# Banded attention with a hand-fixed TensorE order: work moved between ScalarE, VectorE and GpSimd, one PSUM bank used twice, and the theta product started five steps later

## The chip, the cores and the metric

The kernel runs on one core of one Trainium2 chip. The metric is the device time of one execution in microseconds (us). Three runs of the kernel before took 623.08, 624.20 and 625.01 us, so the median is 624.2 us.

Engines are named as the profile names them: PE is TensorE (PEld its weight loads), DVE is VectorE, ACT is ScalarE, POOL is GpSimd, SP is SyncE, which here only issues DMAs.

## The reference

Three blocks run one after the other on batch 2, sequence 768, width 512 (8 heads of 64).

1. Attention: scores = q·kT / 8, kept where the key is one of the first `n_sink` keys (4 here) or lies in the window of the last 128 positions, then softmax, then the product with v. Its output, heads side by side, is x, twelve tiles of 128 rows by 512.
2. Token mixing: theta = x·w_theta; zr = x·cos(theta), zi = x·sin(theta); y = w_tok_r·zr + w_tok_i·zi; u = x + y; u + relu(u·w_ch).
3. The real part of a 2-D Fourier transform of that, added to it, a layer norm, and an MLP of width 2048.

Weights come as 64-bit floats, and the kernel turns their words into 32-bit floats itself. Products that need more than one rounded factor are done as three products of a high and a low part (hi·hi, hi·lo, lo·hi).

## The kernel before

The attention stage (`attn_banded`, L610) is one loop over steps `s`, four per tile of 128 queries (`n, hp = divmod(s, 4)`; twelve tiles, so 48 steps, and a few more for what trails). The loop writes down the order of all work on PE by hand: `strict` (L228) makes every PE instruction follow the one before it in the program. The other engines' queues are ordered by a planner that puts an instruction in its queue when the planner's own clock finds it ready. In one step stand, in this order on PE:

- on even `s` the scores of four heads (`score_mms`, L483), into four PSUM banks; DVE adds the mask and finds the row bound (L515), ACT takes the exponential (L519), and the bank is free again when the exponential has read it;
- on `s % 4 == 2` the product with v of the tile of six steps ago (`av`, L561) into the single bank of the ring `ps_acc` (profile name `oa`), copied to `oT` by ACT (L586);
- for `0 < s < first(0)` two products of a tile of zeros (L641), which nothing reads;
- the transposes of two heads' probabilities (`turn`, L531) into one of the two banks of the ring `ps_tp` (profile name `tp`), copied out in turn by ACT and DVE (L552);
- on `s % 4 == 1`, for tiles that have earlier sink keys, one more transpose: the 16 sink columns of all heads, gathered by a copy `psk` (L524, ACT), also go to a `tp` bank (L555) and are copied to `pst`;
- on `s % 4 == 3` the transpose back of the finished product (`av_turn`, L588), also into a `tp` bank, which DVE reads to normalise (L601);
- parts of `theta_gen` (L776): first four transposes of a finished x tile into a `tp` bank, then twelve products over the following steps into the bank `th`.

`theta_gen` copies its `tp` bank twice on ACT: once rounded to the PE's reduced type (`hi`, L784) and once in full (`xT`, L786). POOL, or DVE for the last tiles, subtracts the two (`lo`, L787). After the products ACT scales the result to turns (`ph`, L798), DVE adds and subtracts a large constant to round to whole turns (`km`, L799 and L800), and POOL subtracts (L801).

Tile u's theta begins at step `first(u) = 4u + 5 + max(4, T0 - u)`. With `T0 = 7` this is 12, 15, 18, 21 and then every fourth step from 25.

The stage also converts weights: at steps 5, 7, 9, 11 (`THS`) the four quarters of w_theta, each split into high and low a step later, and then every third step from 15 to 39 a piece of the token weights (`P0B`, `P0E`, L687). A conversion (`conv`, L269) is one ACT instruction (L281) and three DVE instructions (L289, L290, L293), or, where `low_act` is set, two on ACT (L281, L284) and two on DVE (L285, L293); `low_act` is not set in this stage. Converting a piece also asks SP for the next one. The DMAs of k, q and v are asked for a tile ahead.

After the attention `rest` (L1199) runs the token mixing of the first batch (`y_gen`, from about 168 us in the profile), and then everything else, which the change does not touch.

Of the kernel before, what the change touches and what calls it, by code (L numbers as in the profile page):

```python
# [15 lines left out]
ALU = mybir.AluOpType  # L16
# [5 lines left out]
BLK = 128 + SINK  # L22
PW = 256 + SINK
BIG = 8.0e9
MAGIC = 12582912.0
# [4 lines left out]
GROUPS = [0, 3, 1, 2]  # L30
NSLOT = 67
NSLOT2 = 8
T0 = 7
DEPTH = 3
NRAW = 3
NJIT = 12
# [3 lines left out]
C1E = 12  # L40
TLC = 1
WN = 7
P0B = 15
P0N = 3
P0E = 40
F0 = 0
F1 = 2
ETH = 9
# [3 lines left out]
T1 = 4  # L52
TD = 1
AH = 5
THS = (5, 7, 9, 11)
P1E = 11
P2F = 1
TL = 2
# [132 lines left out]
class _Body:  # L191
# [315 lines left out]
    def scores(self, n, hp):  # L507
        nc = self.nc
        i, c = self.seq[n][1], n % 3
        nb, sm, p = self.tn[n]  # L510
        wd = PW if i else 128
        mask = self.masks[min(i, 2) if c else (0, 1, 3)[min(i, 2)]]
        for u, sc in enumerate(self.scs.pop((n, hp))):
            h = 2 * hp + u
            nc.vector.tensor_tensor_reduce(  # L515
                out=sc[:, 0:wd], in0=sc[:, 0:wd], in1=mask, op0=ALU.add, op1=ALU.min,
                scale=-0.125, scalar=3.0e38, accum_out=nb[:, h:h + 1],
            )
            self.last_exp = nc.scalar.activation(  # L519
                p[:, h, 0:wd], sc[:, 0:wd], AF.Exp, bias=nb[:, h:h + 1], scale=-1.0, accum_out=sm[:, h:h + 1]  # L520
            ).ins
        if hp == 3 and i >= 2:
            psk = self.psk.next()
            self.rnd("a", psk, p[:, :, 128:BLK])  # L524
            self.pt[n, 5] = psk
        if hp == 3:
            q = self.q.pop(n)
            if n:
                self.give(q)

    def turn(self, n, hp):  # L531
        nc = self.nc
        b, i = self.seq[n]
        c = n % 3
        p = self.tn[n][2]
        tp = self.ps_tp.next().rearrange("p (a m) -> p a m", a=4)
        pt = self.take(4, 128)
        parts = []
        for u in range(2):
            x, y = p[:, 2 * hp + u, 0:128], p[:, 2 * hp + u, BLK:PW]  # L540
            if i:
                prev, cur = (x, y) if c else (y, x)
                parts.append((u, prev, n - 1))
                parts.append((u, cur, n))
            else:
                parts.append((u, x, n))
        k = len(parts)
        for a, (u, pp, _) in enumerate(parts):
            self.tr(tp[:, a, :], pp, self.ident)
            yield  # L550
        tail = 4 * n + hp >= 4 * len(self.seq) - 5
        self.ev[n, hp] = self.rnd("v" if tail else EPT[hp], pt[:, 0:k], tp[:, 0:k])  # L552
        self.pt[n, hp] = pt, [(u, m) for u, _, m in parts]
        if hp == 3 and i >= 2:
            tp = self.ps_tp.next()  # L555
            self.tr(tp[:, 0:128], self.pt.pop((n, 5)).rearrange("p h c -> p (h c)"), self.ident)
            pst = self.pst.next()
            self.ev[n, 4] = self.rnd("v" if tail else "a", pst, tp[:, 0:128])
            self.pt[n, 4] = pst
# [26 lines left out]
        self.rnd("a", self.oT, acc)  # L586

    def av_turn(self, n):  # L588
        tp = self.ps_tp.next().rearrange("p (a m) -> p a m", a=4)
        for a in range(4):  # L590
            self.tr(tp[:, a], self.oT[:, a], self.ident)
        self.give(self.oT)
        self.normalize(*self.seq[n], tp.rearrange("p a m -> p (a m)"), self.tn.pop(n)[1])
# [16 lines left out]
    def attn_banded(self):  # L610
        last = len(self.seq) - 1
        nc = self.nc
        self.tn, self.pt, self.scs, self.ev = {}, {}, {}, {}
        th = {}
        self.zth = self.ps_th.tiles[0]
        first = lambda u: 4 * u + AL + 2 + max(T1, T0 - u // TD)
        nstep = 4 * (last + 1)
        for s in range(nstep + T0 + AL + 4):
            n, hp = divmod(s, 4)
            if n < last and hp == 0:  # L620
                b, i = self.seq[n]
                if n:
                    self.load_k(n + 1)
                    self.load_q(n + 1)
                    self.load_v(n + 1)
                if i == NS - 2 and b + 1 < B:
                    self.load_sink(b + 1)
            if s == nstep - 4:
                self.sz = self.s.carve(6)
            if s == AH:  # L630
                self.ahead(2)
            if n <= last and not s % 2:
                self.score_mms(n, hp)
            g, k = divmod(s - AVS, 4)
            if 0 <= g <= last and k == 0:
                self.av(g)
            turn = self.turn(*divmod(s - TL, 4)) if TL <= s < nstep + TL else iter(())
            if 0 < s < first(0):

                for _ in range(2):  # L640
                    i = nc.tensor.matmul(  # L641
                        self.zth[:, 0:256], lhsT=self.zz[:, 0:128], rhs=self.zz, start=s == 1, stop=False,
                        skip_group_check=True,
                    ).ins
                    self.chained(i)
            for _ in turn:
                pass
            g, k = divmod(s - AVS, 4)
            if 0 <= g <= last and k == 1:
                self.av_turn(g)  # L650
            if n <= last and not s % 2:
                self.scores(n, hp)
                self.scores(n, hp + 1)
            if s in (nstep + 1, nstep + 3):
                u = (s - nstep) // 2
                with self.paced(ref=self.ev[last, 0]) if u else self.tc.issue_after(self.last_exp):
                    self.trig_act(0, u)
                with self.paced(ref=self.tl if u else self.ev[last, 1]):
                    self.trig_mul(0, u, "v")
            for u in range(last):  # L660
                k = s - first(u)
                if k == 0:
                    for _ in th.pop(u - 1, ()):
                        pass
                    th[u] = self.theta_gen(*self.seq[u])
                if 0 <= k < 4:
                    next(th[u], None)
            if n < last:
                if s in MST:
                    with self.paced(ref=self.last_exp):  # L670
                        self.build_mask(1 + MST.index(s))
                if s == SKS:
                    with self.paced(ref=self.last_exp):
                        self.sink_cols(0, 0, 1, 2)
                if hp == 0:
                    if n == 1:
                        with self.paced():
                            self.sink_v(0)
                    elif n and self.seq[n][1] == 0:
                        self.sink_cols(b, 0, 1)  # L680
                        self.sink_v(b)
            if s in THS:
                self.pump(0, lag=0, ref=self.last_exp)
            elif s - 1 in THS:
                with self.paced(ref=self.last_exp):
                    self.weight_split("th", THS.index(s - 1))
            elif P0B <= s < P0E and s % P0N == 0:  # L687
                self.pump(12, lag=0, ref=self.last_exp)
            if s - nstep in TAIL:
                u = TAIL.index(s - nstep)  # L690
                with self.paced(ref=self.ev[last, u]):
                    self.weight_split("tok", 1, (0, 2, 1)[u])
                if u < 2:
                    self.pump(8, ref=self.tl)
            if nstep - 4 <= s < nstep - 1:
                with self.paced(ref=self.last_exp):
                    self.weight_split("tok", 0, s - nstep + 4)
        for l in th.values():
            for _ in l:
                pass  # L700
        self.pump(8, ref=self.nrm)
        self.marks, self.strict = [], False
# [73 lines left out]
    def theta_gen(self, b, i):  # L776
        nc = self.nc
# [3 lines left out]
            self.tr(tp[:, a, :], x[:, a * 128:(a + 1) * 128], self.ident)  # L781
        hi = self.take(4, 128, dt=F32R)
        lo = self.take(4, 128, dt=F32R)
        self.rnd("a", hi, tp)  # L784
        xt = self.xT[b][:, :, i * 128:(i + 1) * 128]
        nc.scalar.activation(xt, tp, AF.Copy)  # L786
        self.low("v" if 6 * b + i >= ETH else "p", lo, xt, hi)  # L787
        self.tl = nc.cur_bb.bb.instructions[-1]
        yield
        th = self.ps_th.next()  # L790
# [5 lines left out]
        self.give(hi, lo)  # L796
        ph, km = self.take(512), self.take(512)
        nc.scalar.activation(ph, th, AF.Copy, scale=INV2PI)  # L798
        nc.vector.tensor_scalar(km, ph, MAGIC, None, op0=ALU.add)  # L799
        nc.vector.tensor_scalar(km, km, MAGIC, None, op0=ALU.subtract)  # L800
        nc.gpsimd.tensor_tensor(ph, km, ph, op=ALU.subtract)  # L801
        self.give(km)
        self.ph[b, i] = ph
# [569 lines left out]
```

## Time and profile before

| | value |
|---|---|
| median of three runs | 624.2 us |
| the profiled execution | 624.34 us |
| its span, first to last instruction | 622.6 us |
| PE busy | 587.7 us (94%) |
| DVE busy | 351.0 us (56%) |
| ACT busy | 349.0 us (56%) |
| POOL busy | 299.0 us (48%) |
| mean granted TensorE clock | 0.985 of full |

A row of a window says how long the stretch is, how long each engine was busy in it (with the count of instructions), and the granted clock as a share of full speed (0.50 is 1.2 GHz, 1.00 is 2.4 GHz). A row of the timeline gives start, duration, engine, line, operation and tiles; what stands in square brackets is how long the engine sat idle before it and whose instruction ended that. L206, L207, L211, L221 and L226 are helpers (a copy on ACT, a copy on DVE, a subtraction, a product, a transpose), so there the tile names tell which is which.

### The profile page before, as it was taken

The page shows a single profiled execution, that of the slowest core. Times are in us where ns is not written, and L with a number is a line of the kernel's source. Part 1 is how long each engine was busy: PE and PEld are TensorE (multiplying, and loading weights), DVE is VectorE, ACT ScalarE, POOL GpSimd, SP SyncE. Part 2 cuts the span into 40 slices and gives each one's busy share as a digit, 9 for nine tenths or more (in the row PEclk, how much of TensorE's full clock was granted, in tenths as well). Part 3 has the DMA queues.
Part 4 walks back from the last instruction along what each step waited for, and adds up shares of the span by engine and source line. Part 5 has one row for each costly group of instructions (what it writes and reads, how often), then busy time and mean ns, then how long its engine had stood idle before and what let it go on. Part 6 is the DMA issues. An engine that isn't in the chain of part 4 may idle for free.

```text
span 622.6 us, 9732 instructions
## 1 busy us (share of the span) xinstructions
PE 587.7 (94%) x3586; PEld 511.5 (82%) x3586; DVE 351.0 (56%) x713; ACT 349.0 (56%) x787; POOL 299.0 (48%) x252
## 2 busy tenths in 40 slices
PE   8879999797999999998999999999999999999996
PEld 6647776575787899987899999999898999989995
DVE  5766777667899859896366765548333411121112
ACT  4656657577676554647577775436548534333340
POOL 1121312123367652524665755666856566556551
PEclk9989999799899999999999999999999999999999
DMA  7733433120042722550026652100000100010001
GB/s 245 273 119 99 122 113 109 39 83 1 1 136 69 215 65 68 157 149 1 1 68 204 193 160 88 51 1 1 0 1 4 49 1 1 1 52 1 1 1 57
DMA packets 23338, 46.63 MB, mean 75 GB/s; under 512 B 2512, under 2 KB 9552, under 8 KB 23280
## 3 DMA queue, kind: packets, MB, share of 16 engines
q1 hardware_dynamic: 22032, 43.74, 22.3%
q0 software_dynamic: 1248, 2.17, 1.2%
q8 instruction: 30, 0.49, 0.3%
q14 instruction: 28, 0.23, 0.1%
HBM read 42.75 MB, written 3.15 MB: 74 GB/s over the span
## 4 chain that ended last, share of the span: by engine, by line
PE 61%; DVE 5%; ACT 1%; POOL 1%; issue 0%; POOLq 0%; ACTq 0%
PE pc L221 24%; PE acc L221 20%; PE s L221 8%; PE bank L221 7%; PE s L226 2%; ACT t L206 1%; POOL t L211 1%; DVE t L211 1%; DVE t L1146 0%; DVE t L819 0%; DVE t L987 0%; DVE t L999 0%; ACT t L1068 0%; DVE t L995 0%; DVE t L1053 0%
## 5 line engine op out<-in xcount | busy, mean ns | idle before, releaser
L211 POOL TENSOR_TENSOR t<-t 128x512 fp32r<-128x512 f32 x151 | 203.5, 1367 | 177.6 <-ACT t L206 153.4
L221 PE MATMUL acc<-t 128*128 128x512 f32 x648 | 178.5, 394 | 0.0
L206 ACT ACTIVATE t<-t 128x512 fp32r<-128x512 f32 x172 | 102.4, 626 | 71.5 <-PE acc L221 26.5
L221 PEld LDWEIGHTS acc<-t 128*128 128x128 f32 x648 | 116.5, 188 | 17.8
L221 PE MATMUL pc<-t 128*128 128x384 f32 (+1 forms) x672 | 124.9, 314 | 1.0 <-POOL t L211 0.6
L221 PEld LDWEIGHTS pc<-t 128*128 128x128 f32 x672 | 113.8, 188 | 11.1 <-POOL t L211 0.8
L1133 DVE SCALAR_TENSOR_TENSOR t<-pc,t 128x384 fp32r<-128x384 f32 x64 | 35.6, 557 | 123.9 <-ACT t L1132 123.7
L211 POOL TENSOR_TENSOR t<-xT,t 128x512 fp32r<-128x512 f32 x39 | 52.3, 1359 | 99.6 <-ACT xT L786 61.6
L221 PE MATMUL s<-t 128*128 128x256 f32 (+3 forms) x492 | 70.3, 286 | 1.6 <-DVE st L1053 0.8
L221 PE MATMUL pc<-uh,t 128*128 128x384 f32 x256 | 70.6, 337 | 0.0
L221 PEld LDWEIGHTS s<-t 128*128 128x128 f32 x492 | 65.8, 190 | 4.9 <-DVE st L1053 1.0
L221 PE MATMUL bank<-t 128*128 128x512 f32 x216 | 65.2, 398 | 1.4 <-DVE t L211 1.4
L1132 ACT ACTIVATE t<-pc 128x384 fp32r<-128x384 f32 x64 | 31.3, 489 | 60.8 <-PE pc L221 56.8
L281 ACT ACTIVATE raw<-raw 128x512 f32<-128x512 f32 x58 | 38.8, 674 | 15.1 <-DMA raw<-in_w_ch_dram 9.4
L221 PEld LDWEIGHTS pc<-uh,t 128*128 128x128 f32 x256 | 46.2, 188 | 0.8
L221 PEld LDWEIGHTS bank<-t 128*128 128x128 f32 x216 | 38.7, 188 | 8.0 <-DVE t L211 2.3
L221 PE MATMUL pc<-ul,t 128*128 128x384 f32 x128 | 43.0, 336 | 0.6 <-DVE ul L211 0.6
L519 ACT ACTIVATE p<-sc,nb 128x272 f32<-128x272 f32 (+1 forms) x72 | 33.2, 467 | 16.7 <-DVE nb L515 16.1
L221 PE MATMUL th<-t 128*128 128x512 f32 x132 | 42.5, 438 | 0.0
L515 DVE CUSTOM_DVE_ANT_0 sc<-sc,m 128x272 f32<-128x272 f32 (+1 forms) x72 | 28.9, 442 | 7.4 <-PE sc L221 7.3
L206 ACT ACTIVATE t<-xT 128x512 fp32r<-128x512 f32 x36 | 21.0, 625 | 19.1 <-PE acc L221 7.4
L226 PE MATMUL tp<-ident,p 128*128 128x128 f32 x176 | 29.5, 289 | 2.2 <-ACT t L206 1.8
(142 smaller groups left out, 826.0 us busy)
## 6 DMA issues: line engine op xcount, KB each, us to landing
raw<-in_w_ch_dram SPq DMA_DIRECT2D x36, 512.0 KB, 3.9
kst<-in_k_dram SPq DMA_DIRECT2D x12, 256.0 KB, 3.8
t<-in_v_dram SPq DMA_DIRECT2D x12, 256.0 KB, 4.2
raw<-in_w_tok_rT_dram SPq DMA_DIRECT2D x6, 512.0 KB, 3.6
raw<-in_w_tok_iT_dram SPq DMA_DIRECT2D x6, 512.0 KB, 3.6
out_dram<-t SPq DMA_DIRECT2D x12, 256.0 KB, 2.7
t<-in_q_dram SPq DMA_DIRECT2D x11, 256.0 KB, 3.7
raw<-in_w_theta_dram SPq DMA_DIRECT2D x4, 512.0 KB, 6.0
```

What stands on the lines that cost most here:

```text
L206: return nc.scalar.activation(o, i, AF.Copy).ins
L211: e.tensor_tensor(o, x, hi.bitcast(F32), op=ALU.subtract)
L221: i = self.nc.tensor.matmul(o, lhsT=lhsT, rhs=rhs, start=start, stop=stop, skip_group_check=True).ins
L226: self.chained(self.nc.tensor.transpose(o, x, ident).ins)
L281: nc.scalar.activation(hf, hf, AF.Copy, scale=2.0 ** -112)
L515: nc.vector.tensor_tensor_reduce(out=sc[:, 0:wd], in0=sc[:, 0:wd], in1=mask, op0=ALU.add, op1=ALU.min, scale=-0.125, scalar=3.0e38, accum_ ...
L519: self.last_exp = nc.scalar.activation(p[:, h, 0:wd], sc[:, 0:wd], AF.Exp, bias=nb[:, h:h + 1], scale=-1.0, accum_out=sm[:, h:h + 1]).ins
L1132: nc.scalar.activation(hh, hp, AF.Relu)
L1133: self.hl = nc.vector.scalar_tensor_tensor(hl, in0=hp, scalar=0.0, in1=hh.bitcast(F32), op0=ALU.max, op1=ALU.subtract).ins
```

## The change

- `T0` from 7 to 12: theta of tile u begins at 17, 20, 23, 26, 29, 32, 35, 38, 41, and every fourth step from 45. Tile 0 begins five steps later, tile 7 one step later, tile 8 and those after it as before. The products of zeros run while `s < first(0)`, so through step 16 where it was step 11.
- `THS` to 6, 9, 12, 15; `P0B`, `P0E` to 18 and 43: the nine token pieces are converted at 18 to 42 where it was 15 to 39.
- `low_act` is set for steps below 18, so that the four quarters of w_theta take the form with two ACT and two DVE instructions.
- The sink columns are gathered by POOL where it was ACT.
- The sink transpose and the transpose back take the bank of `ps_acc` where they took one of `ps_tp`.
- For the first nine tiles theta's `hi` is a POOL copy of `xT` where it was an ACT copy of the `tp` bank.
- The rounding to whole turns is one POOL instruction where it was two on DVE.

```diff
-T0 = 7
+T0 = 12
-P0B = 15
+P0B = 18
-P0E = 40
+P0E = 43
-THS = (5, 7, 9, 11)
+THS = (6, 9, 12, 15)
...
-            self.rnd("a", psk, p[:, :, 128:BLK])
+            nc.gpsimd.tensor_copy(psk, p[:, :, 128:BLK])
...
         if hp == 3 and i >= 2:
-            tp = self.ps_tp.next()
+            tp = self.ps_acc.next()
...
     def av_turn(self, n):
-        tp = self.ps_tp.next().rearrange("p (a m) -> p a m", a=4)
+        tp = self.ps_acc.next().rearrange("p (a m) -> p a m", a=4)
...
+            self.low_act = s < P0B
             if s in THS:
...
-        self.rnd("a", hi, tp)
         xt = self.xT[b][:, :, i * 128:(i + 1) * 128]
+        late = 6 * b + i >= ETH
+        if late:
+            self.rnd("a", hi, tp)
         nc.scalar.activation(xt, tp, AF.Copy)
-        self.low("v" if 6 * b + i >= ETH else "p", lo, xt, hi)
+        if not late:
+            nc.gpsimd.tensor_copy(hi, xt)
+        self.low("v" if late else "p", lo, xt, hi)
...
         nc.scalar.activation(ph, th, AF.Copy, scale=INV2PI)
-        nc.vector.tensor_scalar(km, ph, MAGIC, None, op0=ALU.add)
-        nc.vector.tensor_scalar(km, km, MAGIC, None, op0=ALU.subtract)
+        nc.gpsimd.tensor_scalar(km, ph, MAGIC, MAGIC, op0=ALU.add, op1=ALU.subtract)
         nc.gpsimd.tensor_tensor(ph, km, ph, op=ALU.subtract)
```

## Rows read from the trace of the kernel before

**Rows 1.** Windows: attention, two stretches of it at a low clock, and what follows
```profile
7.10:168.20 161.10, 138.63 (x1059) 106.16 (x1058) 114.17 (x334) 104.06 (x313) 37.89 (x31) 0.95 0.34 110
41.00:49.00 8.00, 7.15 (x48) 4.84 (x48) 2.80 (x11) 4.52 (x15) 2.51 (x2) 0.59 0.06 16
113.00:120.00 7.00, 6.73 (x26) 4.72 (x27) 2.55 (x10) 2.72 (x11) 0.00 (x0) 0.55 0.08 30
168.20:200.00 31.80, 30.38 (x169) 25.69 (x168) 31.49 (x38) 22.58 (x42) 21.23 (x13) 1.00 0.32 100
```
**Rows 2.** Waits of PE in attention, the largest: total us, times, longest
```profile
PE tp L226 <- ACT t L206: 18.3, 15, 4.0
```
**Rows 3.** Groups by line and shape, attention: transposes into `tp`; idle before them last
```profile
L226 PE MATMUL tp<-ident,psk 128*128 128x128 f32 x8 | 2.8, 352 | 3.4 <-ACT t L206 2.6 <-ACT xT L786 0.8
L226 PE MATMUL tp<-ident,t 128*128 128x128 f32 x92 | 15.0, 287 | 14.7 <-ACT t L206 13.9 <-ACT xT L786 0.8
```
**Rows 4.** Timeline of PE, five waits in attention
```profile
22.83 0.65 PE L226 MATMUL tp<-ident,t 128*128 128x128 f32 x4 [1.69 <-ACT t L206]
...
28.77 0.95 PE L221 MATMUL sc<-kst,t 64*128 64x272 f32 x5 [1.36 <-ACT p L519]
...
40.93 1.11 PE L226 MATMUL tp<-ident,p 128*128 128x128 f32 x4 [1.80 <-ACT t L206]
...
66.16 0.65 PE L226 MATMUL tp<-ident,t 128*128 128x128 f32 x4 [0.79 <-ACT xT L786]
...
113.27 1.11 PE L226 MATMUL tp<-ident,t 128*128 128x128 f32 x4 [3.40 <-ACT t L206]
```
**Rows 5.** Timeline of ACT: copies of `oT` and of a `tp` bank
```profile
20.17 0.59 ACT L206 ACTIVATE t<-oa 128x512 f32<-128x512 f32 x1
...
22.18 0.60 ACT L206 ACTIVATE t<-tp 128x512 f32<-128x512 f32 x1
...
111.94 0.59 ACT L206 ACTIVATE t<-oa 128x512 f32<-128x512 f32 x1
```
**Rows 6.** Timeline of DVE and POOL ahead of the wait at 113
```profile
107.27 1.30 DVE L800 TENSOR_SCALAR t<-t 128x512 f32<-128x512 f32 x1
...
106.99 1.30 POOL L211 TENSOR_TENSOR t<-xT,t 128x512 fp32r<-128x512 f32 x1 [8.36 <-ACT xT L786]
```
**Rows 7.** Timeline of PE, steps 8 and 9: zeros and transposes
```profile
24.53 1.13 PE L641 MATMUL th<-z 128*128 128x256 f32 x4
25.50 0.60 PE L226 MATMUL tp<-ident,p 128*128 128x128 f32 x4
25.94 1.03 PE L641 MATMUL th<-z 128*128 128x256 f32 x4
26.80 0.60 PE L226 MATMUL tp<-ident,p 128*128 128x128 f32 x4
```
**Rows 8.** Timeline of PE, ACT and POOL: theta of tile 1, three steps behind tile 0
```profile
53.42 0.60 PE L226 MATMUL tp<-ident,t 128*128 128x128 f32 x4
...
55.48 0.94 PE L221 MATMUL th<-t 128*128 128x512 f32 x3
...
54.60 0.60 ACT L786 ACTIVATE xT<-tp 128x512 f32<-128x512 f32 x1
...
55.28 1.39 POOL L211 TENSOR_TENSOR t<-xT,t 128x512 fp32r<-128x512 f32 x1 [10.82 <-ACT xT L786]
```
**Rows 9.** Groups by line and shape: what is moved, and the nearest prices on POOL
```profile
L800 DVE TENSOR_SCALAR t<-t 128x512 f32<-128x512 f32 x10 | 7.9, 792 | 0.0
L799 DVE TENSOR_SCALAR t<-t 128x512 f32<-128x512 f32 x10 | 4.4, 442 | 6.1 <-ACT t L798 6.0
L801 POOL TENSOR_TENSOR t<-t 128x512 f32<-128x512 f32 x10 | 12.7, 1273 | 5.6 <-DVE t L800 4.4 <-PE oa L221 0.8 <-PE tp L226 0.4
L1072 POOL TENSOR_SCALAR rstd<-mv 128x1 f32<-128x1 f32 x12 | 2.3, 190 | 10.2 <-ACT t L1070 7.2 <-ACT mv L1066 1.6 <-ACT xT L1070 0.9
L284 ACT ACTIVATE raw<-raw,below 128x512 int32<-128x512 uint32 x33 | 24.9, 756 | 0.0
```

## The prediction

> **What bounds the kernel now.** I read the windows first, then PE's waits, then the groups by shape, then the timeline around each wait. The reader is to see in the windows that attention runs from 7.1 to 168.2 us, that PE is busy for 138.63 of its 161.10 us, and so idle for 22.5, at a mean granted clock of 0.95 [rows 1]. Behind it PE hardly stops: 30.38 of the next 31.8 us. All that the change touches lies in attention or trails into that stretch, so the question is how much of the 22.5 us, and of what the low clock costs, goes away. The low clock stands in two places above all: 41 to 49 us at 0.59, a loss of 8 × 0.41 = 3.3 us, and 113 to 120 us at 0.55, 7 × 0.45 = 3.2 us [rows 1]; PE had paused 1.80 us just before the first and 3.40 us before the second [rows 4].
>
> The waits say who is late: 18.3 us in 15 pieces, PE's transposes waiting for an ACT copy [rows 2]. By shape it is two kinds: the eight sink transposes 3.4 us, and the transposes of `t` (the transpose back and theta's) 14.7 us [rows 3]. The order on PE is fixed, so one transpose without a bank holds everything behind it. At 22.83 the transpose back starts 1.69 us late; its operand `oT` was copied at 20.17 + 0.59 = 20.76, and what it got at last was the copy of a `tp` bank, at 22.18 + 0.60 = 22.78 [rows 4, 5]. So that wait is for a bank and not for data.
>
> **The change part by part.** The sum is made against the profiled execution, 624.34 us (span 622.6, 1.74 outside it); the median of the runs, 624.2, is the same within 0.14.
>
> *The transposes in the `oa` bank.* The ring `tp` keeps only the probabilities and theta. The sink transpose no longer needs a `tp` bank: 3.4 us gone [rows 3]. The transpose back waits only for `oT`, which it needs anyway. Of the 14.7 us I count whole the waits that were for a bank: 1.69, 0.79 [rows 4] and three more of the latter's pattern, 1.3 together; 3.8 in all. In three others `oT` itself was late, as at 113.27: it was there at 111.94 + 0.59 = 112.53, 0.74 before PE began [rows 4, 5]. About 0.55 each, 1.7. Together 5.5; the longest wait, 4.0 [rows 2], I leave. What does the shared bank cost? `av` writes it again three steps after the transpose back was put there and one step after the sink transpose; scores and a probability transpose stand between them on PE. I take 0; if ACT is late with that copy, `av` stalls, at most as the sink transposes do now (0.4 us each).
>
> *Theta later, its weights spread out, the low word on ACT.* Steps 5 to 11 now hold a conversion every other step, and step 12 theta's first transposes. The wait of 1.36 us for an exponential at 28.77 and the one of 1.80 at 40.93 [rows 4] are of that stretch: 3.2 us. With no theta before step 17 the two `tp` banks serve the probabilities alone, and with them should go the low clock of 41 to 49, 3.3 us. The four quarters cost ACT 4 × 0.756 = 3.0 us more [rows 9], hidden by ACT's idle time (57 of 161 us [rows 1]); uncovered it would be those 3.0. DVE loses one instruction of each. SP's refills move with the conversions; the DMAs are busy for 0.34 of the time [rows 1], so I count nothing.
>
> *Zeros.* Steps 12 to 16 get two products each. In steps 8 and 9 they took 25.50 − 24.53 = 0.97 and 26.80 − 25.94 = 0.86 us of PE [rows 7]. Five steps × 0.92 = 4.6 us **added**; theta's own PE work is only moved, into a phase with a theta every three steps.
>
> *Rounding and `hi` on POOL.* No row has POOL with one input of 128x512. From below 0.19 (128x1), from above 1.27 (two inputs of 128x512) [rows 9]. The nearest in size is the upper one; with one operand less I take the middle, 0.7. DVE gets back 7.9 + 4.4 = 12.3 us in attention [rows 9], ACT nine copies of 0.6 [rows 8] and eight short ones. DVE matters where it delays an exponential and thereby ACT's queue: at 107.27 the second rounding instruction stood 1.30 us, until POOL's at 106.99 ended (its own work is 0.4) [rows 6], then a weight conversion in the same way, and the 3.40 us wait and the low clock followed. What is left of these two is 2.7 + 3.2 = 5.9. A conversion still falls there and POOL is fuller, so I take half: 2.9.
>
> The price is theta's chain. Now the products follow ACT's `hi`; after, ACT's `xT` and then POOL's copy: from the end of the transposes at 54.02 to the end of `xT` at 55.20 it is 1.18, less some 0.5 for the copy of `hi` that stood ahead of it, 0.7; then 0.08 to POOL [rows 8], 0.7 for the copy, 0.08 back: 1.56 us. What PE has to do in that time depends on the step. Transposes at `s % 4 == 1` are followed by scores and `av`: enough. At 3 scores and one transpose, 55.48 − 54.02 = 1.46 [rows 8]: wait 0.1. At 2 two transposes of 0.44 [rows 7]: 0.7. At 0 one and the sink transpose: 1.05. Beginning at 20, 23, 26, 32, 35, 38, theta meets each of these twice: 2 × (0.1 + 0.7 + 1.05) = 3.7 us **added**, with 1.0 (POOL at its lower bound, 0.5 quicker) and 7.1 (at its upper, 0.57 slower) as ends. Thetas 9 to 11 keep ACT's `hi`.
>
> *Density.* Steps 17 to 41 hold more per step. From below 0: a theta three steps behind the one before ran without a wait of PE [rows 8]. From above 4.9, the three early waits again [rows 4]. Nearer to the former, with fuller queues: 2.0 added.
>
> **Sum.** Gone 3.4 + 5.5 + 3.2 + 3.3 + 2.9 = 18.3; added 4.6 + 3.7 + 2.0 = 10.3. Net −8.0: 624.3 − 8.0 = **616 us**. Behind attention I count nothing: DVE is busy 31.49 of 31.80 us there [rows 1], but its work is set off by PE's progress and shifts with it.
>
> **A rule weighed.** At 107.27 a DVE instruction with its operands in SBUF stood until POOL's ended [rows 6], so POOL time is not free for DVE. The Trainium skill, "SBUF — State Buffer", section "Who interferes with whom", calls this an exclusive lock on one pair of ports, which speaks against moving work from DVE to POOL. By that rule the new POOL work shuts DVE out for about as long as DVE is relieved: this is rival 3. On POOL's price the same skill, "GPSIMD Engine Reference", section "4.1 Engine selection", calls one-input work roughly line-rate; by its 1.03 cycles an element (section 3.1) I estimate 0.44 us and a little, which would take some 1 us from the sum; no row here shows it.
>
> **The rivals.**
> 1. *Theta's `hi` late on POOL* (slower). Where a theta begins, POOL gets the rounding and the subtraction of the tile before at the same moment. If the planner puts both ahead of `hi`, it comes 0.7 + 1.27 later, of which 0.5 had passed: about +1.5 at each of six thetas, +8.9. PE then pauses over 2.5 us at steps 20 and 32, and pauses of that kind went ahead of the low clock [rows 1, 4]: +3.2 twice. 616 + 8.9 + 6.4 = 631. It decides from about 1.3 us more per theta (8.0 / 6) on. For: the queue is strictly in order, and `hi` is now on PE's path. Against: at 55.28 POOL, idle for 10.82 us, took the new tile's `lo` first, so ahead of the old tile's subtraction [rows 8].
> 2. *DVE freed for good* (faster). The whole 5.9 us around 113 go, `hi` is hidden behind other waits, and half of the longest wait (4.0 [rows 2]) goes too: 616 − 3.0 − 3.7 − 2.0 = 607. For: DVE's chain led to the wait at 113 [rows 6]. Against: the longest one lies where ACT starts on the sines, and DVE has no part in it.
> 3. *DVE not freed*. New POOL time in attention is 10 × 0.7 + 9 × 0.7 + 8 × 0.35 (half a copy) = 16 us against 12.3 that DVE gets back. Then the 2.9 us stay and about 2 us of new exponential waits come: 621. For: a POOL instruction held DVE for its whole length [rows 6]. Against: it held one whose operands lie in SBUF; DVE's score and copy instructions read PSUM.
> 4. *Given back behind attention*. If DVE's 31.49 of 31.80 us there is a bound of its own, whose start doesn't move, the time stays near 624. Against: PE was idle for only 31.80 − 30.38 = 1.4 us of it.
>
> **How the numbers follow.** About 0.3% (1.9 us) is what a measurement of this kernel can tell from no change. Forecast 0.42 (its own range 611 to 621), rival 1 0.17, rival 2 0.18, rival 3 0.11, rival 4 0.12. Rival 4 is no change; rival 1 and a little of 3 slower; so faster 0.70, same 0.12, slower 0.18. For 8 in 10 I leave out the outer parts of rivals 1 and 2: 605 to 627.
>
> **What would show it.** After: no wait of PE before the sink transposes; the transpose back starting right behind the copy of `oT`; no low clock around 41 us; 64 records of zeros where there were 44; the first theta product at steps 21, 24, 27, 33, 36, 39 waiting for a POOL copy, by 0.1 to 1.05 us each; attention ending near 160. Wrong if POOL's one-input instructions take over 1 us, if PE's waits for POOL sum to more than 8 us, or if the next stage gets longer by what attention loses.

## The result, and the profile after

The changed kernel takes 630.6 us (629.0 to 632.5, four runs) where the kernel before takes 624.5 (623.1 to 625.0). The ratio is 1.0103, with a 95% interval of 1.0070 to 1.0136: slower by 1%, outside the range that was forecast (605 to 627). The profiled execution took 629.0 us, its span is 627.2.

The loss lies in attention and nowhere else. At the end of the first token mixing DVE adds a product to `xT`, four times in a run. The row of these instructions gives shortest, median and longest duration, then the first and the last start. Before:

```profile
L865 DVE TENSOR_TENSOR xT<-pc,xT x4: 679/680/682, 222.8 to 313.7; 128x512 f32<-128x512 f32 x4
```

After, where the line is L869:

```profile
L869 DVE TENSOR_TENSOR xT<-pc,xT x4: 679/680/681, 227.4 to 318.3; 128x512 f32<-128x512 f32 x4
```

The first comes 4.6 us later, and from it to the end of the span it is 399.8 us in both (622.6 − 222.8, 627.2 − 227.4). What follows attention only shifts.

The windows of after, against [rows 1] (duration, busy time of PE, PEld, DVE, ACT and POOL, granted clock, DMA):

```profile
7.10:172.60 165.50, 142.27 (x1071) 109.91 (x1068) 101.13 (x307) 99.16 (x300) 63.52 (x56) 0.95 0.33 108
64.00:71.00 7.00, 6.56 (x42) 4.89 (x43) 2.19 (x10) 2.13 (x9) 3.15 (x4) 0.53 0.41 127
90.00:94.00 4.00, 3.75 (x14) 2.40 (x15) 1.53 (x7) 0.93 (x4) 2.69 (x3) 0.63 0.18 70
111.00:115.00 4.00, 3.17 (x11) 2.02 (x11) 0.45 (x2) 0.00 (x0) 3.26 (x4) 0.57 0.38 131
```

Attention is 4.4 us longer although DVE has 13 us less to do in it and ACT 5 us less; POOL has 26 us more. PE is idle for 23.2 us, where it was 22.5. The low clock hasn't gone but moved: 41 to 49 us runs at full speed now, and 64 to 71, 90 to 94 and 111 to 115 don't.

PE's waits in attention, against [rows 2], say what took the place of ACT:

```profile
PE th L221 <- POOL t L791: 13.8, 6, 3.4
PE tp L226 <- ACT t L206: 4.2, 3, 1.8
PE oa L226 <- ACT t L206: 2.4, 1, 2.4
PE sc L221 <- ACT p L519: 2.2, 2, 1.4
PE oa L221 <- DVE t L207: 0.3, 1, 0.3
```

The 18.3 us for ACT's copies fell to 6.6 (4.2 + 2.4). In their stead stand six waits of theta's products (`th`) for POOL's L791, which is the copy that makes `hi`. The groups of transposes, against [rows 3], show that the part with the banks did what it says: no wait is left before the sink transposes, and the transposes of `t`, now half in `oa` and half in `tp`, wait for 5.3 us where it was 14.7 (the busy time comes first, the idle time before the group behind the second bar).

```profile
L226 PE MATMUL oa<-ident,t 128*128 128x128 f32 x44 | 6.8, 278 | 2.6 <-ACT t L206 2.4
L226 PE MATMUL tp<-ident,t 128*128 128x128 f32 x44 | 6.7, 275 | 2.7 <-ACT t L206 2.7
L226 PE MATMUL oa<-ident,psk 128*128 128x128 f32 x8 | 2.2, 272 | 0.0
```

Now one theta, that of tile 1, in the timeline of after: PE, ACT and POOL.

```profile
59.92 0.60 PE L226 MATMUL tp<-ident,t 128*128 128x128 f32 x4
...
64.44 1.65 PE L221 MATMUL th<-t 128*128 128x512 f32 x3 [3.34 <-POOL t L791]
...
61.17 0.61 ACT L803 ACTIVATE t<-th 128x512 f32<-128x512 f32 x1
61.65 0.62 ACT L789 ACTIVATE xT<-tp 128x512 f32<-128x512 f32 x1
...
61.88 1.94 POOL L804 TENSOR_SCALAR t<-t 128x512 f32<-128x512 f32 x1 [7.92 <-ACT t L803]
63.78 0.60 POOL L791 CAST t<-xT 128x512 fp32r<-128x512 f32 x1
64.36 1.26 POOL L805 TENSOR_TENSOR t<-t 128x512 f32<-128x512 f32 x1
65.58 1.28 POOL L211 TENSOR_TENSOR t<-xT,t 128x512 fp32r<-128x512 f32 x1
```

`xT` is there at 61.65 + 0.62 = 62.27 and POOL's copy needs 0.60, so `hi` could be there before 63. But ACT gave POOL tile 0's `ph` 0.5 us earlier, and POOL began its rounding (L804), which lasts 1.94 us. `hi` starts at 63.78, right behind it, and PE at 64.44. The same four instructions in the same order stand at each of the eight thetas of tiles 1 to 8 (at tile 8 a `psk` copy stands between them); PE waits at six of them, and at tiles 4 and 8 it doesn't. The rounding is not the whole wait: behind a free POOL `hi` would have started 0.07 us after `xT` (run 3 below has 62.88 and 62.95), at 62.34, so 1.4 of the 3.34 us are the queue's. Over the six waits this makes 8.4 of the 13.8 us (an estimate from the starts of the copies). The rest is the longer path over `xT`, which was late itself: its transposes ended at 59.92 + 0.60 = 60.52, and ACT had an exponential, an instruction of a weight conversion and `ph` ahead of it. The prices on POOL, over the whole run:

```profile
L804 POOL TENSOR_SCALAR t<-t 128x512 f32<-128x512 f32 x12 | 24.6, 2047 | 44.9 <-ACT t L803 44.9
L805 POOL TENSOR_TENSOR t<-t 128x512 f32<-128x512 f32 x12 | 16.8, 1404 | 0.2
L791 POOL CAST t<-xT 128x512 fp32r<-128x512 f32 x9 | 5.5, 607 | 0.6 <-ACT xT L789 0.6
L524 POOL COPY psk<-p 128x128 f32<-128x128 f32 x8 | 2.3, 291 | 20.6 <-ACT p L519 20.5
```

The copies cost a little less than was taken (0.61 for 0.7, 0.29 for 0.35). The rounding costs 2.05 us where 0.7 was taken, and lies outside the bounds that [rows 9] gave, 0.19 to 1.27.

### The profile page after: what moved, and what is told of

Read it like the earlier page. It is cut to its first block, busy times and chain, and to the rows that moved or that the text cites. A ratio compares the mean times of both kernels' runs of the same rounds, so it can differ in the third digit from the quotient of the medians.

```text
span 627.2 us, 9817 instructions
## 1 busy us (share of the span) xinstructions
PE 591.7 (94%) x3606; PEld 516.1 (82%) x3606; DVE 339.7 (54%) x685; ACT 344.0 (55%) x774; POOL 331.1 (53%) x281
## 4 chain that ended last, share of the span: by engine, by line
PE 73%; DVE 10%; ACT 8%; issue 3%; DMA 2%; POOL 2%; SPq 0%; ACTq 0%; DVEq 0%; POOLq 0%
PE pc L221 24%; PE acc L221 21%; PE s L221 8%; PE bank L221 8%; PE th L221 3%; ACT p L519 3%; PE oa L221 2%; ACT t L206 2%; PE s L226 2%; PE tp L226 2%; PE sc L221 2%; DMA raw<-in_w_theta_dram 1%; DVE t L211 1%; DVE t L823 1%; POOL t L804 1%
## 5 line engine op out<-in xcount | busy, mean ns | idle before, releaser
L211 POOL TENSOR_TENSOR t<-t 128x512 fp32r<-128x512 f32 x151 | 202.7, 1363 | 172.1 <-ACT t L206 145.5
L211 POOL TENSOR_TENSOR t<-xT,t 128x512 fp32r<-128x512 f32 x39 | 52.6, 1367 | 27.8 <-ACT t L206 27.7
L221 PE MATMUL th<-t 128*128 128x512 f32 x132 | 41.9, 440 | 13.9 <-POOL t L791 13.8
L804 POOL TENSOR_SCALAR t<-t 128x512 f32<-128x512 f32 x12 | 24.6, 2047 | 44.9 <-ACT t L803 44.9
L221 PEld LDWEIGHTS th<-t 128*128 128x128 f32 x132 | 23.8, 202 | 18.6 <-POOL t L791 15.6
```

The lines of the kernel that those rows point to most:

```text
L211: e.tensor_tensor(o, x, hi.bitcast(F32), op=ALU.subtract)
L221: i = self.nc.tensor.matmul(o, lhsT=lhsT, rhs=rhs, start=start, stop=stop, skip_group_check=True).ins
L804: nc.gpsimd.tensor_scalar(km, ph, MAGIC, MAGIC, op0=ALU.add, op1=ALU.subtract)
```

## The experiments

The theory from here on is *the queue*: `hi` stands behind a 2 us rounding in POOL's queue, PE's fixed order waits for it, and behind the pause the clock is low. Its rivals are *POOL's load* (its new instructions shut DVE out, wherever they stand) and *the schedule* (theta every three steps, more products of zeros). Each run is compared with the kernel before on the same chip (624.1 to 625.2 us); the changed kernel is the 630.6 us above.

**1. `hi` on ACT again, all else as changed.**

```diff
-        if late:
-            self.rnd("a", hi, tp)
+        self.rnd("a", hi, tp)
         nc.scalar.activation(xt, tp, AF.Copy)
-        if not late:
-            nc.gpsimd.tensor_copy(hi, xt)
```

> The changed kernel with one part undone: theta's high part is again an ACT copy of the transposes' bank. Queue theory (the 2 us rounding stands ahead of the high part in POOL's queue, and PE waits for it): the 13.8 us of PE's waits for POOL go, and most of the 6 us of low clock behind them; some of it comes back as other waits, so 614 to 619 us. Rival 'POOL's load' (its 25 us of rounding shut DVE out): the rounding stays, so at least 627. Rival 'schedule' (theta every three steps and ten more products of zeros cost it): at least 627.

608.4 us, ratio 0.9742 (0.9714 to 0.9770). One copy per theta on the other engine is worth 22 us, and without it the change is a gain of 16; that is more than the queue expected (614 to 619). The waits of PE:

```profile
PE oa L226 <- ACT t L206: 3.0, 2, 2.4
PE tp L226 <- ACT t L206: 2.6, 2, 1.8
PE th L221 <- ACT t L206: 2.5, 2, 1.3
PE sc L221 <- ACT p L519: 1.9, 3, 1.0
PE s L226 <- DVE t L601: 0.5, 1, 0.5
```

The windows from 62 to 122 us and from 122 to 150 here, and then the first of them in the changed kernel:

```profile
62.00:122.00 60.00, 57.12 (x455) 44.61 (x456) 39.21 (x124) 39.80 (x125) 30.89 (x24) 1.00 0.32 102
122.00:150.00 28.00, 25.55 (x218) 20.67 (x217) 19.85 (x48) 22.78 (x55) 17.23 (x14) 0.94 0.06 20
```

```profile
62.00:122.00 60.00, 48.32 (x337) 36.49 (x337) 30.39 (x91) 26.53 (x85) 26.14 (x23) 0.89 0.25 82
```

POOL is busier here than in the changed kernel (30.89 against 26.14 us), with PE at 57.12 of 60 us and the full clock. POOL's load and the schedule are both refuted as the main cause: both are in this kernel, but for the 5.5 us of POOL's copies themselves. The first `xT<-pc` comes at 206.3 us of a span of 606.3, so 400.0 us before the end: the gain too is attention's alone. Of all the kernels run here this one (with run 7, which is the same within the measurement) is the fastest, and the version to keep.

**2. The rounding back on DVE, `hi` on POOL.**

```diff
-        nc.gpsimd.tensor_scalar(km, ph, MAGIC, MAGIC, op0=ALU.add, op1=ALU.subtract)
+        nc.vector.tensor_scalar(km, ph, MAGIC, None, op0=ALU.add)
+        nc.vector.tensor_scalar(km, km, MAGIC, None, op0=ALU.subtract)
```

> The changed kernel with the rounding back on DVE in two instructions; the high part stays on POOL. Queue theory: PE's waits for POOL fall from 13.8 us to the 3.7 that were forecast with a free POOL; 617 to 622 us. POOL's load: 25 us less of it, 617 to 622 as well (the next run tells these two apart). Schedule: at least 627.

618.2 us, ratio 0.9899 (0.9871 to 0.9927), as the queue and the load expected. The waits for POOL halve, to 6.5 us (3.7 were expected):

```profile
PE th L221 <- POOL t L791: 6.5, 5, 2.8
PE oa L226 <- ACT t L206: 4.5, 2, 3.6
```

**3. The same instructions on the same engines, in another order.** The rounding and subtraction of a theta are issued behind the next theta's `lo`:

```diff
+        self.whole(self.tl if not late else None)
         yield
         th = self.ps_th.next()
...
-        nc.gpsimd.tensor_scalar(km, ph, MAGIC, MAGIC, op0=ALU.add, op1=ALU.subtract)
-        nc.gpsimd.tensor_tensor(ph, km, ph, op=ALU.subtract)
-        self.give(km)
+        self.turns.append((ph, km))
+        if late:
+            self.whole()
...
+    def whole(self, ref=None):
+        nc = self.nc
+        while self.turns:
+            ph, km = self.turns.pop()
+            r = nc.gpsimd.tensor_scalar(km, ph, MAGIC, MAGIC, op0=ALU.add, op1=ALU.subtract).ins
+            if ref is not None:
+                self.after(r, ref)
+            nc.gpsimd.tensor_tensor(ph, km, ph, op=ALU.subtract)
+            self.give(km)
```

> The changed kernel with the same instructions on the same engines, but the rounding and subtraction of a theta put into POOL's queue behind the high and low part of the next. Queue theory: as with the rounding on DVE, 616 to 622 us, PE's waits for POOL under 5 us. POOL's load: unchanged, 628 to 633. Schedule: 628 to 633.

617.2 us, ratio 0.9869 (0.9823 to 0.9914): 13.4 us from order alone, with the same instructions on POOL. POOL's queue at tile 1's theta, in this kernel, where L792 is `hi`, L211 is `lo` and L816 the rounding:

```profile
62.95 1.09 POOL L792 CAST t<-xT 128x512 fp32r<-128x512 f32 x1 [9.98 <-ACT xT L790]
64.12 1.61 POOL L211 TENSOR_TENSOR t<-xT,t 128x512 fp32r<-128x512 f32 x1
65.72 1.94 POOL L816 TENSOR_SCALAR t<-t 128x512 f32<-128x512 f32 x1
```

The queue's number for PE's waits was missed: 6.3 us for POOL, where under 5 was expected. And 617.2 is 8.8 above the kernel with `hi` on ACT. The profiled execution took 620.0 us, and in 62 to 122 us its clock is 0.89 too, a loss of 60 × 0.11 = 6.6 us. The four times make two pairs: 615.0 us twice, at a mean granted clock of 0.994 and 0.996 over the whole run, and 619.4 and 620.0 at 0.986 and 0.985. The profile is of the slower pair, so what made the difference stays open, and so do the 6.6 us by which even they are slower than run 1, but for the longer path over `xT` (3.6 us by runs 2 and 5).

**4. The banks and the sink columns alone, on the kernel before.** Old steps, `hi` on ACT, rounding on DVE.

```diff
-            self.rnd("a", psk, p[:, :, 128:BLK])
+            nc.gpsimd.tensor_copy(psk, p[:, :, 128:BLK])
...
-            tp = self.ps_tp.next()
+            tp = self.ps_acc.next()
...
-        tp = self.ps_tp.next().rearrange("p (a m) -> p a m", a=4)
+        tp = self.ps_acc.next().rearrange("p (a m) -> p a m", a=4)
```

> The kernel before with the transposes in the oa bank and the sink columns on POOL alone; old schedule, the high part on ACT, the rounding on DVE. The sum of the prediction: 3.4 and 5.5 us of bank waits gone, 615 to 618 us. Schedule rival: this is the fastest of the four, below the one with the high part on ACT by more than 3 us. If the bank waits were hidden by other waits: 622 to 625.

614.7 us, ratio 0.9838 (0.9803 to 0.9872): 10.2 us less than before, where the forecast had 8.9 for this part (so just under the 615 to 618 expected). As the schedule's rival lost (the first run is 6.3 us faster than this one), the rest was taken apart.

**5. `hi` on ACT and the rounding on DVE, banks and schedule as changed** (the edits of 1 and 2 together).

> The changed kernel with both the high part on ACT and the rounding on DVE in two instructions; banks, sink columns and schedule as changed. It tells what the rounding on POOL is worth once PE doesn't wait behind it (608.4 us with it). If freeing DVE pays: 611 to 615, with exponentials waiting for DVE again. If POOL's 2 us roundings shut DVE out as much as they free it: 607 to 610. If they cost: below 607.

614.6 us, ratio 0.9829 (0.9800 to 0.9858). It lies in the range for "freeing DVE pays": against run 1 the rounding on POOL is worth 6.2 us. In 62 to 122 us DVE is busy 5.9 us longer than in run 1, and PE less:

```profile
62.00:122.00 60.00, 55.32 (x443) 43.08 (x441) 45.10 (x136) 41.41 (x127) 18.10 (x16) 1.00 0.33 103
```

**6. `hi` on ACT, rounding on POOL, the old steps** (`T0 = 7`, `THS = (5, 7, 9, 11)`, `P0B = 15`, `P0E = 40`, `low_act` off, on top of 1).

> High part on ACT, rounding and sink columns on POOL, the banks as changed, but theta and the weight conversions at the old steps and the low word on DVE. It tells what the schedule is worth (608.4 with it, 614.7 without it and with the rounding on DVE). If the schedule gains: 612 to 616, with the low clock near 41 us back. If the 10 products of zeros and the denser phase cost what the forecast took (4.6 and 2.0): 604 to 607.

609.3 us, ratio 0.9755 (0.9729 to 0.9781). Between this and run 1 there is 0.8 us, between 4 and 5 0.1: the schedule is worth nothing that these runs can tell. 609.3 lies between the two ranges that were expected, so both had the schedule wrong.

**7. `hi` on ACT, and no more zeros behind step 11.**

```diff
-            if 0 < s < first(0):
+            if 0 < s < min(12, first(0)):
```

> High part on ACT, all else as changed, but the products of zeros end at step 11 and theta still begins at 17. The forecast charged 4.6 us for the ten products of steps 12 to 16. If that PE time is on the path: 604 to 605. If without it PE waits for the exponentials in the same steps instead: 608. If the clock falls for want of PE work there: 609 to 614, with a granted clock under 0.9 between 35 and 62 us.

608.4 us, ratio 0.9734 (0.9702 to 0.9766), the same as run 1. The time of the products that go comes back, most of it as waits (PE's waits in attention sum to 14.0 us, 10.5 in run 1) and some of it in the clock (0.97 up to 62 us, 1.00 in run 1). One such wait of PE (timeline), which run 1 doesn't have:

```profile
36.99 0.99 PE L221 MATMUL sc<-kst,t 64*128 64x288 f32 x5 [1.55 <-ACT p L519]
```

**8. The rounding on POOL as two instructions of one operation, `hi` on POOL.**

```diff
-        nc.gpsimd.tensor_scalar(km, ph, MAGIC, MAGIC, op0=ALU.add, op1=ALU.subtract)
+        nc.gpsimd.tensor_scalar(km, ph, MAGIC, None, op0=ALU.add)
+        nc.gpsimd.tensor_scalar(km, km, MAGIC, None, op0=ALU.subtract)
```

> The changed kernel (high part on POOL) with the rounding still on POOL but as two instructions of one operation each instead of one of two. It measures the price of one. If a one-operation instruction costs about as much as the copy of the same size (0.6 us), two make 1.2, PE's waits for POOL fall from 13.8 to 6 to 9 us and the time to 619 to 626. If each costs 2 us as the two-operation one does, the waits grow by six times 2 us: 640 or more. If each costs 1 us: 630.

630.8 us, ratio 1.0100 (1.0073 to 1.0128). The two instructions by line:

```profile
L804 POOL TENSOR_SCALAR t<-t 128x512 f32<-128x512 f32 x12 | 19.4, 1616 | 38.4 <-ACT t L803 38.4
L805 POOL TENSOR_SCALAR t<-t 128x512 f32<-128x512 f32 x12 | 18.7, 1562 | 0.2
```

One operation with a constant costs 1.6 us here, two in one instruction 2.05, and a cast of the same size 0.61 (the last two in the changed kernel). None of the three expectations has this number; the nearest (1 us each, 630) has the time. Together they are 3.2 us against 2.05, yet PE's waits for POOL fell a little, to 11.8 us, because the planner put `hi` between the two. POOL at tile 1's theta, in this kernel:

```profile
61.64 1.52 POOL L804 TENSOR_SCALAR t<-t 128x512 f32<-128x512 f32 x1 [7.93 <-ACT t L803]
63.12 0.87 POOL L791 CAST t<-xT 128x512 fp32r<-128x512 f32 x1
63.96 1.49 POOL L805 TENSOR_SCALAR t<-t 128x512 f32<-128x512 f32 x1
```

So `hi` stood behind 1.5 us here and not behind 1.9. The time did not fall with these waits, as other waits of PE grew (those for DVE's copies to 2.6 us from 0.3): in attention they sum to 23.7 us, 22.9 in the changed kernel.

**9. Products of zeros in PE's pauses.** On the changed kernel, ahead of the first product of the thetas of tiles 1 to 8; eight of them, and in a later run four.

```diff
         th = self.ps_th.next()
+        if 0 < 6 * b + i < ETH and self.strict:
+            for z in range(8):
+                self.chained(nc.tensor.matmul(
+                    th[:, 0:256], lhsT=self.zz[:, 0:128], rhs=self.zz, start=z == 0, stop=False,
+                    skip_group_check=True,
+                ).ins)
```

> The changed kernel with eight products of zeros (1.75 us of PE) ahead of each theta's first product for tiles 1 to 8, where PE waits for the high part. It tells the waits from the low clock behind them. If about a third of the 22 us is low clock that follows a pause: the waits shrink to under 2 us each, no stretch falls under 0.8 of the clock between 62 and 122 us, and the time comes down to 624 to 628 although the work grows by 14 us of products. If the clock has no part in it: the products cost what they don't hide, 631 to 638.

632.6 us, ratio 1.0123 (1.0094 to 1.0152). By its letter this is the range for a clock without a part (631 to 638). But the expectation was built on a wrong price: eight products take 3.4 us and not 1.75, so 27 us of products went in, and the ranges decide nothing. What the run does say points the other way: 27 us of products came and 13.8 us of waits for POOL went, which alone would add 13 us; it is 2.0 us, and the clock in 62 to 122 us is 1.00. With four:

> The changed kernel with four products of zeros ahead of each theta's first product for tiles 1 to 8. Eight took 3.4 us each time (twice what was reckoned), so four take 1.7: 13.6 us of products in all, of which the waits for POOL (1.06 to 3.42 us at six places) can hide 6 x about 1.6 = 9.6. If the low clock that follows a pause costs some 6 us of the 22 and goes with the pauses: 630.6 + 13.6 - 9.6 - 6 = 628 to 629, no stretch under 0.9 of the clock between 62 and 122 us. If the clock costs nothing: 634 to 635.

623.2 us, ratio 0.9971 (0.9956 to 0.9987). The changed kernel with 13.6 us of useless PE work added is 7.4 us **faster** than without, and 5 us faster than expected with a part for the clock (628 to 629). The waits for POOL and the windows of this run, where attention ends 5.5 us sooner, at 167.1 (the first `xT<-pc` comes at 221.9):

```profile
PE th L221 <- POOL t L791: 2.2, 4, 0.6
```

```profile
7.10:167.10 160.00, 150.04 (x1139) 118.24 (x1138) 101.27 (x307) 99.09 (x300) 63.56 (x56) 0.99 0.34 111
62.00:122.00 60.00, 56.68 (x414) 43.91 (x414) 33.96 (x101) 29.43 (x95) 30.37 (x26) 1.00 0.24 80
```

POOL is as late as ever (at tile 1 `hi` starts 1.5 us after `xT` here too); PE merely doesn't stand still while it is, and the clock stays at full speed. Attention of the profiled execution is 160.0 us, 5.5 less than in the changed kernel. PE's idle time in it went from 23.2 to 10.0 us, 13.2 less, and 13.6 us of products came, so 5.9 us are left by which PE's own work got shorter. The low clock in 62 to 122 us, which is gone here, cost 60 × 0.11 = 6.6 us (0.89 in the changed kernel's window shown under experiment 1), so the clock is enough to explain it.

**10. `hi` and rounding on POOL, the old steps** (the five settings of run 6 on the changed kernel).

> The changed kernel with theta and the conversions at the old steps (every fourth step from tile 4 on, where scores and a product with v stand between a theta's transposes and its first product); high part and rounding on POOL. Queue theory: only tiles 1 to 3 are three steps behind the one before, so PE's waits for POOL fall from 13.8 to 5 to 8 us, and the time is 614 to 620, where the same schedule with the high part on ACT took 609.3. If the cost of the high part on POOL doesn't hang on the spacing: 630.

618.8 us, ratio 0.9900 (0.9872 to 0.9928). The waits for POOL, 5.7 us, are where they were expected:

```profile
PE tp L226 <- ACT t L206: 6.3, 4, 1.8
PE th L221 <- POOL t L791: 5.7, 5, 2.1
```

With `hi` on ACT the same schedule took 609.3, so `hi` on POOL costs 9.5 us here and 22 with the new steps. Not because POOL is free: at tiles 1 to 8 `hi` stands behind the rounding of the tile before at the old steps too, and starts 1.5 to 2.0 us after `xT`. At tile 4, ACT, POOL and PE:

```profile
85.75 0.63 ACT L789 ACTIVATE xT<-tp 128x512 f32<-128x512 f32 x1
...
85.99 2.23 POOL L804 TENSOR_SCALAR t<-t 128x512 f32<-128x512 f32 x1 [4.16 <-ACT t L803]
88.17 0.61 POOL L791 CAST t<-xT 128x512 fp32r<-128x512 f32 x1
...
85.97 1.97 PE L221 MATMUL oa<-t 128*64 128x128 f32 x32
...
89.00 0.94 PE L221 MATMUL th<-t 128*128 128x512 f32 x3
```

`hi` is there at 88.78, and PE, which had scores and the product with v to do in between, takes it at 89.00 without a wait. The new steps, free by themselves, begin six thetas where PE has only two transposes, or scores and one transpose, to do in between, and there the same delay becomes PE's.

## Why the prediction was wrong

*The step that failed* is the one headed "Rounding and `hi` on POOL", and in it the term of 3.7 us for theta's chain. It took 0.7 us for any one-input instruction and let POOL be free when `xT` comes. Alone that term has the right size: with the rounding on DVE, `hi` on POOL costs 618.2 − 614.6 = 3.6 us (runs 2 and 5). That is in part luck: PE's waits for POOL were 6.5 us there, up to 2.8, and not 3.7, up to 1.05; but 2.9 us of waits for `hi` stand in run 5 too, where ACT makes it. But the rounding went to the same queue, took 2.05 us, and was given to POOL 0.5 us ahead of `xT` each time. The six waits came to 13.8 us, 1.06 to 3.42 each, where 0.1 to 1.05 were forecast, and behind three of them the clock was low (from 64, 90 and 111 us on). On and off ACT, that one copy is 22 us by the medians, and 20.9 between the spans of the two profiles (627.2 and 606.3). Of these 20.9, waits of theta's products, 13.8 against 2.5 us, make 11.3; the clock, 0.95 of 165.5 us and so 8.3 against 1.7 (28 us at 0.94 in run 1), 6.6; some 3 are not assigned.

*The bounds* were the deeper error. Both were rows of POOL and looked safe: a tiny instruction of the same kind below, a bigger kind of the same size above. The instruction lay above both. (The lower end of the term is also summed wrong: 0.5 us off each of 0.1, 0.7 and 1.05, none below 0, leaves 2 × (0 + 0.2 + 0.55) = 1.5 and not 1.0. The 616 doesn't hang on it.) The Trainium skill, "GPSIMD Engine Reference", section "4.1 Engine selection", puts one-input work at roughly line-rate; the cast (0.61 us, where the prediction estimated 0.44 and a little from that page) comes near it, the arithmetic with constants (1.6 and 2.05 us) doesn't, and the measurement decides.

*Rival 1* had the mechanism, the place and nearly the time: 631 for 630.6. It had the waits at 3.7 + 8.9 = 12.6 us (13.8) and the clock at 6.4 (6.6). One part of it was not so: the subtraction stayed behind `hi`, only the rounding went ahead; that its 1.94 us came to the 0.7 + 1.27 that the two were to take is luck, and the time to within 1 us with it. It was given 0.17. The argument against it, that POOL took the new tile's `lo` first [rows 8], was read from a kernel in which POOL had nothing to do between `ph` and `lo`, because DVE did the rounding.

*The other terms.* The banks: 8.9 forecast, 10.2 measured (run 4). The schedule: 3.2 + 3.3 gained and 4.6 + 2.0 added, so nothing in sum; nothing measured (6 against 1, 5 against 4). But 4.6 us for the zeros is wrong as a term of its own: they run where PE would wait (run 7). The rounding off DVE: 2.9 forecast, 5.5 to 6.2 measured (4 against 6, 5 against 1), once nothing stands behind it. *Rival 2*'s 607 is what the change gives without the copy on POOL (608.4). *Rival 3*, DVE shut out, is refuted by runs 1 and 5: with the rounding on POOL DVE is busy less by 5.9 us in 62 to 122, and the kernel is 6.2 us faster. *Rival 4* is refuted by the 400 us that follow attention in every kernel here (399.5 to 400.2 from the first `xT<-pc` to the end of the span).

*The signs listed:* the sink transposes wait no more; the transpose back starts right behind the copy of `oT` in the common case (20.07 + 0.60 on ACT, 20.73 on PE); no low clock around 41; 64 records of zeros; waits at the six steps named, but 13.8 us of them where 3.7 were said. Attention ends 12.6 us later than the 160 forecast. Two of the three conditions under which the forecast was to be wrong came true: a one-input instruction over 1 us, and over 8 us of waits for POOL.

The rows of that common case, ACT and then PE of the changed kernel, against [rows 4, 5]:

```profile
20.07 0.60 ACT L206 ACTIVATE t<-oa 128x512 f32<-128x512 f32 x1
...
20.73 0.66 PE L226 MATMUL oa<-ident,t 128*128 128x128 f32 x4
```

## What to carry to other kernels

When two pieces of work move to the same idle engine, price the pair and not each by itself: ask what stands in that queue at the moment when the piece that somebody waits for arrives, for work that nobody waits for paid there (the rounding, 6 us gained) and a link of PE's chain behind it did not (`hi`, 22 us lost, 3.6 without the rounding ahead of it). Whether a late link costs anything is decided by what the waiting engine has left to do at that step: with other steps the same delay on POOL cost 9.5 us. Where PE's order is fixed, a wait is priced with the clock behind it (here 11.3 us of waits came with 6.6 us of low clock). A bound for an instruction that no row shows, taken from another operation or another size, is a guess: here both bounds were such, and the price lay above them.

## What the runs showed of the hardware that was not expected

- On POOL, 128x512 fp32, means in these kernels: a cast to the reduced type 0.61 us, a subtraction of two tiles 1.27 (before) to 1.40 (after), one operation with a constant 1.6 (run 8), two operations with constants in one instruction 2.05. The one-input arithmetic is dearer here than the two-input one.
- PE work that nobody reads can pay: four products of zeros (1.7 us) in each of eight places made the changed kernel 7.4 us faster, with PE's waits for POOL down from 13.8 to 2.2 us and the granted clock at 1.00 in 62 to 122 us (0.89 without them). Eight in each place (3.4 us) also held the clock at 1.00, but made it 2.0 us slower.
